# Half tiles of the gate phases: three excursions in the first and last block, and the shape of PV beside PV

## The chip, the cores and the metric

The kernel runs on one core of one Trainium2 chip, as one launch. The metric is device time in microseconds (us) of one execution, as the median of several runs. TensorE does the matmuls, VectorE (DVE) and ScalarE (ACT) read its results from PSUM, GpSimd (POOL) masks and scales in SBUF, and SyncE (SP) issues most of the DMAs.

## The reference

The input has 2048 tokens of 448 features. They are normalised once, and two branches read the result: causal attention in a sliding window of 256 with 16 heads of 28 features, and a gated feed-forward part with 1792 hidden features. Both are added to the input.

```python
xn = _layernorm(x, axis=-1)
return x + _A_ref(xn, A_wqkv, A_wo) + _B_ref(xn, B_w_gate, B_w_up, B_w_down)

# A: q, k, v = xn @ wqkv, by heads; scores = q k^T * Dh ** -0.5, masked to 0 <= i - j < 256
#    softmax(scores) @ v, by heads, then @ wo
# B: (gelu(xn @ w_gate) * (xn @ w_up)) @ w_down
```

## The kernel before

The tokens are cut into four blocks of 512 (`qb` 0 to 3). Each block has an attention phase and then a gate phase, in the order of the program; every engine runs its own instructions strictly in that order. In an attention phase, scores, exponentials and PV (the product of the probabilities with v, L560) are mixed by hand-written feeds with other dense work: the projections of the next block (`gen_proj`), the output products of the block before (`gen_down`), and in blocks 0 and 3 some of the up products ahead of time (`gen_up`). Which pairs are done ahead stands in `early`: f = 2, 4, 8 in block 0, and 2, 4, 6, 8, 10 in block 3; none in blocks 1 and 2.

The gate phase (`gated`, L412) goes over the 14 slices of 128 hidden features in pairs f = 0, 2, ..., 12. The 448 input features are 3 x 128 + 64. So a product of a slice is three dense matmuls (`three`, L228, array shape 128x128) and one half tile over the last 64 features (`half`, `mm_half`, L233, array shape 64x128). Half tiles come in pairs, one on the upper and one on the lower 64 rows of the array, which run at the same time. A pair f that is not early has two gate products and two up products, and so four half tiles; an early pair has only its gate products, two half tiles. To go from dense matmuls to half tiles and back is called an excursion here. To have few of them, the half tiles of two pairs are put together: `a`, whose dense part has just been issued, ends with its half tiles (`stop`), and `b` begins with them (`start`) and does its dense part afterwards.

```python
for fs in ((0,), (2, 4), (6, 8), (10, 12)):
    a = begin(fs[0])
    dense(a, True)
    ...
    halves(a, False)
    if b: halves(b, True)
    else: last_v()
    end(a)
```

So there are four excursions in a block: f = 0 alone, followed by the block's last PV (`last_v`, which is `rest` of `attention` and calls `pv(3)`), then 2 and 4, 6 and 8, 10 and 12. PV runs in array shape 64x32 in blocks 1 to 3 (48 matmuls, eight places of the array), and in 128x32 in block 0. Its result goes to SBUF through `add_halves` in blocks 1 to 3 (a copy on ScalarE, L548, and an addition on VectorE, L549), and through one copy on VectorE in block 0 (L570).

`end` applies Gelu on ScalarE to the two gate products at once (L452, tile `gt`, two banks) and multiplies with the up products on VectorE (L456, or L454 where they are already in `hT`). It then calls `hook`, which places other work behind each pair: the sums and scalings of the last heads (`after`), and in blocks 0 and 1 the normalisation of later tokens with their DMA transposes, and DMAs of packed k rows.

PSUM has eight banks. In the gate phase two tiles of two banks each (pool tag "s") take turns for `gt`, and four single banks (tags "m" twice, "o", "d") hold the up products and PV's result. A tile is taken again only when its reader is done: with the two `gt` tiles, a pair waits for the Gelu of the pair before the last. `turn` gives the order in which "o" and "d" are used, and `last_tag` hands it on to the output products that follow.

Of the kernel before, what the change touches and what calls it, by code (L numbers as in the profile page):

```python
# [8 lines left out]
ACT = mybir.ActivationFunctionType  # L9
ALU = mybir.AluOpType  # L10
AX = mybir.AxisListType
bf16 = mybir.dt.bfloat16
f32 = mybir.dt.float32
# [3 lines left out]
P = 128  # L17
NT = S // P
NF = F // P
QB, NB = 512, 4  # L20
# [55 lines left out]
def kernel(  # L76
# [11 lines left out]
    nc = tc.nc  # L88
# [6 lines left out]
    psum = fast.enter_context(tc.tile_pool(name="psum", bufs=2, space=bass.MemoryType.PSUM))  # L95

    phase = [None]
# [82 lines left out]
    xnT = const.tile([P, 4, S], bf16, name="xnT")  # L180
# [47 lines left out]
            nc.tensor.matmul(ps, lhsT=lhs(c), rhs=rhs(c), start=start and c == 0, stop=stop and c == 2,  # L228
                             skip_group_check=True)

    def mm_half(ps, lhs, rhs, hi, start, stop):
        p0 = 64 * hi
        nc.tensor.matmul(ps, lhsT=lhs[p0:p0 + 64], rhs=rhs[p0:p0 + 64], start=start, stop=stop,  # L233
                         tile_position=(p0, 0), skip_group_check=True)

    done = set()
    ring = [("m", "m", "d"), 0]
# [11 lines left out]
    def v_half(t, pv):  # L249
        mm_half(pv, xnT[:, 3, t * P:(t + 1) * P], wv[:, 3, :], t % 2, False, True)  # L250
# [22 lines left out]
    def qk_halves(qb, g, pq, pk):  # L273
        w3 = w3p[:, 4 * g:4 * g + 4, :].rearrange("p h d -> p (h d)")
        for hi, ps in enumerate((pq, pk)):
            mm_half(ps, w3, xnT[:, 3, qb * QB:(qb + 1) * QB], hi, False, True)
# [108 lines left out]
        hT = blk.tile([P, NF, QB], bf16, name="hT", tag="hT")  # L385
        hTs[qb] = hT

    def half(ps, f, gate, hi, ts, start, stop):

        w3 = wgu3 if gate != bool(hi) else wug3  # L390
        mm_half(ps, w3[:, f * P:(f + 1) * P], xnT[:, 3, ts], hi, start, stop)

    def three(ps, f, gate, ts, start, stop):
        w = wg if gate else wu
        mm3(ps, lambda c: w[:, c, f * P:(f + 1) * P], lambda c: xnT[:, c, ts], start, stop)

    def gen_up(qb, fs):

        ts = slice(qb * QB, (qb + 1) * QB)
        for f in fs:  # L400
            us = []
            for i in range(2):
                us.append(bank("ue"))
                three(us[i][:, :], f + i, False, ts, True, False)
                yield (650, HOLD) if i else 650
            for i in range(2):
                half(us[i][:, :], f + i, False, i, ts, False, True)
            for i in range(2):
                nc.vector.tensor_copy(out=hTs[qb][:, f + i, :], in_=us[i][:, :])  # L409
            yield -360  # L410

    def gated(qb, early, last_v, hook):  # L412

        ts = slice(qb * QB, (qb + 1) * QB)
        hT = hTs[qb]
        turn = ["o" if down_tag[0] == "d" else "d", down_tag[0]] * 4

        def begin(f):
            last_tag[0] = turn[0] if f not in early else last_tag[0]
            pr = dict(f=f, gt=phase[0].pool.tile([P, 2, QB], f32, name="gt", tag="s"), us=[])  # L420
            if f not in early:
                alone = (turn.pop(0), 1)
                tags = (("m", 2), alone)
                if qb == 0 and f == 0:
                    nxt = [ring[0][(ring[1] + i) % 3] for i in range(2)]
                    tags = [(x, 2 if x == "m" else 1) for x in nxt]
                    if "d" in nxt:
                        turn.insert(0, "o")
                for tag, n in tags:
                    pr["us"].append(psum.tile([P, QB], f32, name="u0", tag=tag, bufs=n))  # L430
            return pr

        def dense(pr, start):
            f = pr["f"]
            gs = [(pr["gt"][:, i, :], f + i, True) for i in range(2)]
            us = [(u[:, :], f + i, False) for i, u in enumerate(pr["us"])]
            for ps, fi, gate in (gs + us if f else us + gs):
                three(ps, fi, gate, ts, start, not start)

        def halves(pr, start):  # L440
            f = pr["f"]
            for i in range(2):
                if pr["us"]:
                    half(pr["gt"][:, i, :], f + i, True, 0, ts, start, not start)
                    half(pr["us"][i][:, :], f + i, False, 1, ts, start, not start)
                else:
                    half(pr["gt"][:, i, :], f + i, True, i, ts, start, not start)

        def end(pr):
            f = pr["f"]  # L450
            ge = work.tile([P, 2, QB], bf16, name="ge", bufs=2)
            nc.scalar.activation(out=ge[:, :, :], in_=pr["gt"][:, :, :], func=ACT.Gelu_apprx_tanh)  # L452
            if not pr["us"]:
                nc.vector.tensor_tensor(out=hT[:, f:f + 2, :], in0=ge[:, :, :], in1=hT[:, f:f + 2, :], op=ALU.mult)  # L454
            for i, u in enumerate(pr["us"]):
                nc.vector.tensor_tensor(out=hT[:, f + i, :], in0=ge[:, i, :], in1=u[:, :], op=ALU.mult)  # L456
            hook(f)

        for fs in ((0,), (2, 4), (6, 8), (10, 12)):
            a = begin(fs[0])  # L460
            dense(a, True)
            b = begin(fs[1]) if len(fs) > 1 else None
            halves(a, False)
            if b:
                halves(b, True)
            else:
                last_v()
            end(a)
            if b:
                dense(b, False)  # L470
                end(b)

    def steps_of(qb):

# [266 lines left out]
    for qb in range(NB):  # L741
# [13 lines left out]
        else:  # L755
            ring[0] = ("m",)
            tags = "dodo" if last_tag[0] == "o" else "odod"
# [16 lines left out]
        def hook(f):  # L774
            after(f)
            if qb < 3 and f == 4:
                collect(qb + 1)
            if qb < 3 and f == 10:
                deliver(qb + 1)
            if f >= 4 and qb < 2:  # L780
                t = 4 * qb + 4 + f // 2
                if f < 12:
                    norm(t + 2)
                    dma_transp(t + 2)
                    if qb == 0:
                        stat(t + 6)

        gated(qb, early, rest, hook)
        if qb < NB - 1:
            nc.scalar.preload_act_table_set("natural_log_exp_and_others")  # L790
# [138 lines left out]
```

## Time and profile before

| | |
|---|---|
| median of 3 runs | 223.92 us (223.68 to 224.28) |
| profiled execution | span 222.5 us from first to last instruction; no other time is recorded for it |
| mean granted clock of TensorE | 0.994 |
| TensorE matmuls | 2215, busy 211.6 us |
| TensorE weight loads | 2240, busy 94.5 us, beside matmuls |
| VectorE | 370 instructions, busy 156.3 us |
| ScalarE | 129 instructions, busy 132.9 us |
| GpSimd | 65 instructions, busy 44.7 us |
| gate phases | about 38.2 to 56.3 (block 0), 84.9 to 108 (1), 136 to 160 (2), 188 to 203.3 (3) |

Matmuls overlap one another: a dense one over 512 columns is listed with 0.38 us, and the next one starts before it has ended. So what counts is the distance from start to start, and not the length. Some records of matmuls are missing in a trace; a row then has a smaller count than the program and a gap of one matmul. Times inside the profile are counted from the first instruction.

### The profile page before, as it was taken

How to read it: one execution, taken by the hardware profiler on the slowest of the kernel's cores; microseconds unless marked ns; L12 is line 12 of the kernel's file. 1: busy time of each engine (PE TensorE's matmuls, PEld its weight loads, DVE VectorE, ACT ScalarE, POOL GpSimd, SP SyncE). 2: the span in 40 equal slices, each digit the busy share in tenths (PEclk: the TensorE clock that was granted, in tenths of full speed). 3: DMA queues.
4: the chain of work that ended last, by engine and by line, in shares of the span. 5: the costliest groups of instructions: out<-in, count | busy, mean ns of one | idle time of the engine just before them, and what ended most of it. 6: DMA issues, size and time to landing. Idle time of an engine off the chain costs nothing.

```text
span 222.5 us, 5330 instructions
## 1 busy us (share of the span) xinstructions
PE 211.6 (95%) x2215; PEld 94.5 (42%) x2240; DVE 156.3 (70%) x370; ACT 132.9 (60%) x129; POOL 44.7 (20%) x65
## 2 busy tenths in 40 slices
PE   6899999999999999999999999999999999999990
PEld 2333333344444454444444445444444435434470
DVE  5989996799666983778566895585454999479210
ACT  4597788644878874533868886323767778453000
POOL 5763687320000220022000030022000022022000
PEclk9999999999999999999999999999999999999997
DMA  6994899104100001001500001200000000000011
GB/s 190 312 327 47 195 327 289 20 2 72 45 3 21 24 24 31 16 19 28 70 0 24 24 0 45 43 0 0 0 4 24 24 0 24 21 0 4 22 45 27
DMA packets 18046, 13.31 MB, mean 60 GB/s; under 512 B 8704, under 2 KB 16992, under 8 KB 18016
## 3 DMA queue, kind: packets, MB, share of 16 engines
q1 hardware_dynamic: 17072, 12.62, 21.6%
q8 instruction: 19, 0.31, 0.6%
q10 hardware_dynamic: 944, 0.29, 0.5%
q14 instruction: 11, 0.09, 0.2%
HBM read 9.15 MB, written 2.18 MB: 51 GB/s over the span
## 4 chain that ended last, share of the span: by engine, by line
PE 91%; DVE 4%; issue 1%; DMA 1%; ACT 0%; DVEq 0%
PE po L375 20%; PE gt L228 17%; PE u L228 12%; PE sc L600 6%; PE po L370 6%; PE gt L233 5%; PE ue L228 5%; PE ov L560 5%; PE pq L228 4%; PE pv L228 4%; PE pk L228 3%; PE pq L233 2%; DVE st L195 1%; PE ue L233 1%; DMA x_sb<-in_A_x_dram 1%
## 5 line engine op out<-in xcount | busy, mean ns | idle before, releaser
L604 ACT ACTIVATE p_sb<-sc 128x2048 bf16<-128x2048 f32 (+2 forms) x42 | 73.8, 1758 | 12.6 <-PE sc L600 7.3
L375 PE MATMUL po<-wd,hT 128*128 128x448 bf16 (+1 forms) x238 | 50.0, 342 | 0.0
L452 ACT ACTIVATE ge<-gt 128x1024 bf16<-128x1024 f32 x28 | 28.7, 1024 | 33.6 <-PE u L233 20.9
L527 POOL TENSOR_TENSOR oN<-oc,l 128x512 bf16<-128x512 f32 x12 | 16.0, 1333 | 138.6 <-DVE l L544 88.2
L228 PE MATMUL gt<-xnT,wg 128*128 128x512 bf16 x161 | 38.9, 380 | 1.0 <-issue 0.9
L456 DVE TENSOR_TENSOR hT<-ge,u 128x512 bf16<-128x512 bf16 x40 | 25.6, 682 | 9.7 <-ACT ge L452 9.6
L375 PEld LDWEIGHTS <-hT 128*128 128x128 bf16 x238 | 21.4, 98 | 18.6 <-issue 2.6
L228 PE MATMUL u<-xnT,wu 128*128 128x512 bf16 x116 | 28.8, 379 | 0.2
L508 DVE TENSOR_TENSOR p_sb<-p_sb,masks 128x256 bf16<-128x256 bf16 (+1 forms) x90 | 27.2, 356 | 0.4 <-ACT p_sb L604 0.4
L228 PEld LDWEIGHTS <-wg 128*128 128x128 bf16 x168 | 15.1, 98 | 21.5 <-issue 5.2
L228 PEld LDWEIGHTS <-wu 128*128 128x128 bf16 x168 | 16.0, 98 | 19.2 <-issue 1.0
L549 DVE TENSOR_TENSOR oc<-oc,ov 128x512 f32<-128x512 f32 x12 | 8.3, 688 | 18.3 <-ACT oc L548 18.3
L600 PE MATMUL sc<-qT,kT 28*64 28x320 bf16 (+7 forms) x640 | 16.9, 263 | 0.1
L380 DVE TENSOR_TENSOR res<-po,x_sb 128x448 bf16<-128x448 f32 (+1 forms) x17 | 9.9, 585 | 8.7 <-PE po L375 8.6
L370 PE MATMUL po<-wo,oN 128*128 128x448 bf16 (+1 forms) x68 | 15.9, 343 | 0.0
L518 POOL TENSOR_SCALAR_AFFINE_SELECT p_sb<-p_sb 128x512 bf16<-128x512 bf16 (+1 forms) x20 | 14.2, 731 | 8.3 <-ACT p_sb L604 8.1
L409 DVE CAST hT<-ue 128x512 bf16<-128x512 f32 x16 | 10.2, 680 | 6.3 <-PE ue L233 6.2
L548 ACT COPY oc<-ov 128x512 f32<-128x512 f32 x12 | 7.0, 584 | 11.9 <-PE ov L560 11.9
L233 PE MATMUL gt<-xnT,wgu 64*128 64x512 bf16 x48 | 13.2, 379 | 0.0
L228 PE MATMUL pq<-xnT,wqp 128*128 128x512 bf16 x36 | 11.7, 380 | 0.7 <-DVE v_sb L253 0.3
L534 DVE STREAM_TRANSPOSE l<-oc 128x512 f32<-128x512 f32 x16 | 11.3, 704 | 1.4 <-POOL oN L527 1.2
L228 PE MATMUL ue<-xnT,wu 128*128 128x512 bf16 x43 | 11.6, 380 | 0.4 <-issue 0.2
(87 smaller groups left out, 235.4 us busy)
## 6 DMA issues: line engine op xcount, KB each, us to landing
out_dram<-res SPq DMA_DIRECT2D x15, 112.0 KB
x_sb<-in_A_x_dram SPq DMA_DIRECT2D x3, 448.0 KB
wu<-in_B_w_up_dram SPq DMA_DIRECT2D x1, 1344.0 KB
wg<-in_B_w_gate_dram SPq DMA_DIRECT2D x1, 1344.0 KB
wd<-in_B_w_down_dram SPq DMA_DIRECT2D x3, 448.0 KB
wraw<-in_A_wqkv_dram SPq DMA_DIRECT2D x2, 252.0 KB
wo<-in_A_wo_dram SPq DMA_DIRECT2D x4, 98.0 KB
wv<-in_A_wqkv_dram SPq DMA_DIRECT2D x1, 336.0 KB
```

What stands on the lines that cost most here:

```text
L228: nc.tensor.matmul(ps, lhsT=lhs(c), rhs=rhs(c), start=start and c == 0, stop=stop and c == 2, skip_group_check=True)
L233: nc.tensor.matmul(ps, lhsT=lhs[p0:p0 + 64], rhs=rhs[p0:p0 + 64], start=start, stop=stop, tile_position=(p0, 0), skip_group_check=True)
L370: nc.tensor.matmul(po[:, 0:w], lhsT=oN[:, g, cs], rhs=wo[:, g, lo:up], start=(g == 0), stop=False, skip_group_check=True)
L375: nc.tensor.matmul(po[:, 0:w], lhsT=hT[:, f, cs], rhs=wd[:, f, lo:up], start=False, stop=(f == NF - 1), skip_group_check=True)
L452: nc.scalar.activation(out=ge[:, :, :], in_=pr["gt"][:, :, :], func=ACT.Gelu_apprx_tanh)
L456: nc.vector.tensor_tensor(out=hT[:, f + i, :], in0=ge[:, i, :], in1=u[:, :], op=ALU.mult)
L508: nc.vector.tensor_tensor(out=reg, in0=reg, in1=m, op=ALU.mult)
L518: nc.gpsimd.affine_select(out=reg, in_=reg, pattern=mid + [[1 if diag else -1, min(w, P)]], compare_op=ALU.is_ge, fill=0.0, base=0 if diag ...
L527: nc.gpsimd.tensor_tensor(out=oN[:, g, :], in0=oc[:, :], in1=inv, op=ALU.mult)
L534: nc.vector.transpose(out=l1[:, :, :].rearrange("p a b -> p (a b)"), in_=oc[:, :])
L600: nc.tensor.matmul(ss[k0:k0 + nk, j, col:col + nq], lhsT=kT[r, g, kt * P + k0:kt * P + k0 + nk], rhs=qT[r, g, qb * QB + q0:qb * QB + q0 + ...
L604: nc.scalar.activation(out=p_sb[:, :, 0:ncol], in_=ss[:, :, 0:ncol], func=ACT.Exp, scale=SCALE)
```

## The change

In blocks 0 and 3 the pairs are grouped as (0, 2), (4, 8, 6), (10, 12), which makes three excursions; blocks 1 and 2 keep their four. In a group of three the middle one (f = 8, early in both blocks) takes two single banks for its gate products in place of a `gt` tile (`apart`), and its Gelu is two instructions of one bank each. The half tiles of the group that stands beside PV (f = 0, and f = 2 with it in block 3) are issued in blocks 1 to 3 as four matmuls of 32 columns each, which is PV's array shape 64x32; in block 0 they keep 64x128. The order of the pairs, and with it of `hook`, becomes 0, 2, 4, 8, 6, 10, 12 in blocks 0 and 3.

```diff
-    def mm_half(ps, lhs, rhs, hi, start, stop):
+    def mm_half(ps, lhs, rhs, hi, start, stop, m=P):
         p0 = 64 * hi
-        nc.tensor.matmul(ps, lhsT=lhs[p0:p0 + 64], rhs=rhs[p0:p0 + 64], start=start, stop=stop,
-                         tile_position=(p0, 0), skip_group_check=True)
+        for c in range(0, P, m):
+            nc.tensor.matmul(ps[c:c + m], lhsT=lhs[p0:p0 + 64, c:c + m], rhs=rhs[p0:p0 + 64], start=start, stop=stop,
+                             tile_position=(p0, c), skip_group_check=True)
...
+        def single(name, tag):
+            return psum.tile([P, QB], f32, name=name, tag=tag, bufs=2 if tag == "m" else 1)[:, :]
+
-        def begin(f):
+        def begin(f, apart=False):
             last_tag[0] = turn[0] if f not in early else last_tag[0]
-            pr = dict(f=f, gt=phase[0].pool.tile([P, 2, QB], f32, name="gt", tag="s"), us=[])
+            pr = dict(f=f, us=[])
+            if apart:
+                pr["gs"] = [single("g0", tag) for tag in ("m", turn.pop(0))]
+                return pr
+            pr["gt"] = phase[0].pool.tile([P, 2, QB], f32, name="gt", tag="s")
+            pr["gs"] = [pr["gt"][:, i, :] for i in range(2)]
...
         def end(pr):
             f = pr["f"]
             ge = work.tile([P, 2, QB], bf16, name="ge", bufs=2)
-            nc.scalar.activation(out=ge[:, :, :], in_=pr["gt"][:, :, :], func=ACT.Gelu_apprx_tanh)
+            if "gt" in pr:
+                nc.scalar.activation(out=ge[:, :, :], in_=pr["gt"][:, :, :], func=ACT.Gelu_apprx_tanh)
+            else:
+                for i, g in enumerate(pr["gs"]):
+                    nc.scalar.activation(out=ge[:, i, :], in_=g, func=ACT.Gelu_apprx_tanh)
...
-        for fs in ((0,), (2, 4), (6, 8), (10, 12)):
-            a = begin(fs[0])
-            dense(a, True)
-            b = begin(fs[1]) if len(fs) > 1 else None
-            halves(a, False)
-            if b:
-                halves(b, True)
-            else:
+        for fs in ((0, 2), (4, 8, 6), (10, 12)) if qb in (0, 3) else ((0,), (2, 4), (6, 8), (10, 12)):
+            prs = [begin(fs[0])]
+            dense(prs[0], True)
+            prs += [begin(f, len(fs) == 3 and f == fs[1]) for f in fs[1:]]
+            for pr in prs:
+                halves(pr, pr is not prs[0], 32 if qb and not fs[0] else P)
+            if not fs[0]:
                 last_v()
-            end(a)
-            if b:
-                dense(b, False)
-                end(b)
+            end(prs[0])
+            for pr in prs[1:]:
+                dense(pr, False)
+                end(pr)
```

More of the change, by code (lines that the diff above doesn't have):

```diff
@@ L386, in new_hT, with half @@
         hTs[qb] = hT
-    def half(ps, f, gate, hi, ts, start, stop):
+    def half(ps, f, gate, hi, ts, start, stop, m=P):
         w3 = wgu3 if gate != bool(hi) else wug3
-        mm_half(ps, w3[:, f * P:(f + 1) * P], xnT[:, 3, ts], hi, start, stop)
+        mm_half(ps, w3[:, f * P:(f + 1) * P], xnT[:, 3, ts], hi, start, stop, m)
     def three(ps, f, gate, ts, start, stop):
@@ L416, in gated @@
         turn = ["o" if down_tag[0] == "d" else "d", down_tag[0]] * 4
-        def begin(f):
+        def single(name, tag):
+            return psum.tile([P, QB], f32, name=name, tag=tag, bufs=2 if tag == "m" else 1)[:, :]
+        def begin(f, apart=False):
             last_tag[0] = turn[0] if f not in early else last_tag[0]
-            pr = dict(f=f, gt=phase[0].pool.tile([P, 2, QB], f32, name="gt", tag="s"), us=[])
+            pr = dict(f=f, us=[])
[4 more added lines that the diff above has]
+            pr["gs"] = [pr["gt"][:, i, :] for i in range(2)]
             if f not in early:
-                alone = (turn.pop(0), 1)
-                tags = (("m", 2), alone)
+                tags = ("m", turn.pop(0))
                 if qb == 0 and f == 0:
-                    nxt = [ring[0][(ring[1] + i) % 3] for i in range(2)]
-                    tags = [(x, 2 if x == "m" else 1) for x in nxt]
-                    if "d" in nxt:
+                    tags = [ring[0][(ring[1] + i) % 3] for i in range(2)]
+                    if "d" in tags:
                         turn.insert(0, "o")
-                for tag, n in tags:
-                    pr["us"].append(psum.tile([P, QB], f32, name="u0", tag=tag, bufs=n))
+                pr["us"] = [single("u0", tag) for tag in tags]
             return pr
@@ L434, in dense, with halves @@
             f = pr["f"]
-            gs = [(pr["gt"][:, i, :], f + i, True) for i in range(2)]
-            us = [(u[:, :], f + i, False) for i, u in enumerate(pr["us"])]
+            gs = [(g, f + i, True) for i, g in enumerate(pr["gs"])]
+            us = [(u, f + i, False) for i, u in enumerate(pr["us"])]
             for ps, fi, gate in (gs + us if f else us + gs):
                 three(ps, fi, gate, ts, start, not start)
-        def halves(pr, start):
+        def halves(pr, start, m):
             f = pr["f"]
@@ L443, in halves @@
                 if pr["us"]:
-                    half(pr["gt"][:, i, :], f + i, True, 0, ts, start, not start)
-                    half(pr["us"][i][:, :], f + i, False, 1, ts, start, not start)
+                    half(pr["gs"][i], f + i, True, 0, ts, start, not start, m)
+                    half(pr["us"][i], f + i, False, 1, ts, start, not start, m)
                 else:
-                    half(pr["gt"][:, i, :], f + i, True, i, ts, start, not start)
+                    half(pr["gs"][i], f + i, True, i, ts, start, not start, m)
         def end(pr):
@@ L455, in end @@
             for i, u in enumerate(pr["us"]):
-                nc.vector.tensor_tensor(out=hT[:, f + i, :], in0=ge[:, i, :], in1=u[:, :], op=ALU.mult)
+                nc.vector.tensor_tensor(out=hT[:, f + i, :], in0=ge[:, i, :], in1=u, op=ALU.mult)
             hook(f)
-        for fs in ((0,), (2, 4), (6, 8), (10, 12)):
-            a = begin(fs[0])
-            dense(a, True)
-            b = begin(fs[1]) if len(fs) > 1 else None
-            halves(a, False)
-            if b:
-                halves(b, True)
-            else:
+        for fs in ((0, 2), (4, 8, 6), (10, 12)) if qb in (0, 3) else ((0,), (2, 4), (6, 8), (10, 12)):
[5 more added lines that the diff above has]
+            if not fs[0]:
                 last_v()
-            end(a)
-            if b:
-                dense(b, False)
-                end(b)
+            end(prs[0])
+            for pr in prs[1:]:
+                dense(pr, False)
+                end(pr)
     def steps_of(qb):
```

## Prediction

> **What bounds the kernel now.** I read the page first: the engine totals, then the chain that ended last.
>
> ```profile
> PE 211.6 (95%) x2215; PEld 94.5 (42%) x2240; DVE 156.3 (70%) x370; ACT 132.9 (60%) x129; POOL 44.7 (20%) x65
> ...
> PE 91%; DVE 4%; issue 1%; DMA 1%; ACT 0%; DVEq 0%
> ```
>
> TensorE is busy for 95% of the span and is 91% of the chain, so a tenth of a microsecond taken from its queue moves the end by as much, unless a wait takes its place. The change edits only that queue's order and shapes in the gate phases, so next I read the timeline of TensorE through block 3's gate phase (start us, length us, line, output and inputs, array shape, moving shape, count), and after it ScalarE's rows of the same stretch.
>
> ```profile
> 189.25 1.46 PE L228 MATMUL gt<-xnT,wg 128*128 128x512 bf16 x6
> 190.64 0.39 PE L233 MATMUL gt<-xnT,wgu 64*128 64x512 bf16 x1
> ...
> 190.87 0.38 PE L233 MATMUL gt<-xnT,wgu 64*128 64x512 bf16 x1
> ...
> 191.18 0.74 PE L560 MATMUL ov<-p_sb,v_sb 64*32 64x256 bf16 x48
> 192.08 1.24 PE L228 MATMUL gt<-xnT,wg 128*128 128x512 bf16 x5 [0.16 <-issue]
> 193.25 0.39 PE L233 MATMUL gt<-xnT,wgu 64*128 64x512 bf16 x1
> ...
> 193.66 0.37 PE L233 MATMUL gt<-xnT,wgu 64*128 64x512 bf16 x1
> ...
> 193.98 2.76 PE L228 MATMUL gt<-xnT,wg 128*128 128x512 bf16 x12
> 196.68 0.39 PE L233 MATMUL gt<-xnT,wgu 64*128 64x512 bf16 x1
> ...
> 196.91 0.38 PE L233 MATMUL gt<-xnT,wgu 64*128 64x512 bf16 x1
> ...
> 197.22 2.76 PE L228 MATMUL gt<-xnT,wg 128*128 128x512 bf16 x12
> ```
>
> ```profile
> 192.10 0.58 ACT L548 COPY oc<-ov 128x512 f32<-128x512 f32 x1 [2.91 <-PE ov L560]
> 192.58 2.13 ACT L452 ACTIVATE ge<-gt 128x1024 bf16<-128x1024 f32 x2
> ```
>
> The pitch of dense matmuls is (2.76 - 0.38)/11 = 0.216 us. Anything beyond one pitch between starts is a switch of array shape or a wait. Twelve dense matmuls from 193.98 would be followed at 193.98 + 12 x 0.216 = 196.57; the half tiles start at 196.68, 0.10 late. Two half tiles run abreast in a pitch: two pairs are 0.43, and the next dense one starts at 197.22 where 196.57 + 0.43 = 197.00 was due. So **one excursion of half tiles costs about 0.21 us** besides its work, some 0.10 at each end.
>
> From the last pair (190.87) to PV (191.18) is 0.31: **the switch from 64x128 to PV's 64x32 costs 0.09**. The 192.08 row holds five of the six matmuls of f=2 (one record is missing), so the first stood a pitch earlier, at 191.86.
>
> One real wait stands in this phase: the second pair at 193.66 comes 0.41 after the first, 0.41 - 0.22 = 0.19 late. It is f=4's first use of the two-bank tile that f=0's Gelu must leave, and that Gelu stands on ScalarE behind the copy of PV's result: PV starts at 191.18, the copy at 192.10, and f=0's Gelu runs to about 193.6 (two Gelus of 1.02 with a pause between). **The tile is free 193.66 - 191.18 = 2.48 after PV's start.**
>
> **The change part by part.**
>
> *Block 0, three excursions.* The half tiles of f=0 and f=2 now share one excursion, followed by PV as before; f=4, 8, 6 share the next; f=10, 12 stay. One excursion goes: -0.21. I looked for a wait in its place. Here the result of PV is copied by VectorE, so ScalarE runs f=0's Gelu ahead of it, as this view of the same stretch of block 0 shows:
>
> ```profile
> 41.58 1.02 ACT L452 ACTIVATE ge<-gt 128x1024 bf16<-128x1024 f32 x1 [0.89 <-PE gt L233]
> 42.60 0.69 DVE L570 COPY oc<-ov 128x512 f32<-128x512 f32 x1 [1.39 <-POOL oN L527]
> 43.21 1.27 DVE L456 TENSOR_TENSOR hT<-ge,u 128x512 bf16<-128x512 bf16 x2
> ```
>
> f=4's dense part would start about 43.5 (f=2's start at 42.02 in the trace, plus one pair 0.22, plus six pitches 1.30), and its tile is free at 42.6: no wait. From there in pitches: f=4 dense to 44.8, the switch 0.1, half tiles of f=4 (0.22), f=8 at 45.1, f=6 at 45.4 (two pairs, 0.43); dense f=8 from 45.9 to 47.2, f=6 (twelve, 2.59) to 49.8, f=10 to 52.4; half tiles of f=10 from 52.5, of f=12 at 52.9, its second pair at 53.1. f=8's two single banks, PV's old one among them (copied by 43.3), and f=6's banks, f=0's old ones (free with the products at 44.5), are there in time. The tightest is f=12, which takes f=6's banks: VectorE does f=8's product (0.65), norm (0.60) and statistics (0.62 + 0.18) from about 49.0 to 51.0, then f=6's two products (1.28) to 52.3, and the second bank is wanted at 53.1. Margin 0.8; if that cover went, by VectorE being as much as one such round of 1.4 late, the loss would be 0.6. Splitting f=8's Gelu in two adds one ScalarE start, at most 2 x 0.58 - 1.02 = 0.14 by the copy of one bank, beside dense work. The DMAs issued in hook keep their order but for tokens 9 and 10 exchanged; token 9's transpose goes out near 53 rather than 51, and TensorE wants it at 58.6: nothing. Value -0.21; bounds -0.21 and +0.4.
>
> *Blocks 1 and 2, half tiles in 64x32.* Four matmuls become sixteen, 24 added in the two blocks. No row shows 64x512 in this shape. The nearest is PV: 48 matmuls, in sum 10,240 columns, which eight abreast at the pitch's rate (0.216/512) are 0.54; from its start 191.18 to the next dense matmul at 191.86 are 0.68, and 0.14 of that is the drain out. So PV runs eight abreast, and 16 x 512/8 columns are 0.43, as now. The switch of 0.09 goes: -0.09 a block, -0.18 for both. Bounds: -0.20 (a little skew saved too) and, four abreast, +0.43 - 0.09 = +0.34 a block.
>
> *Block 3, both.* One excursion fewer, -0.21, and 64x32 for the 24 matmuls of f=0 and f=2, -0.09: -0.30. But **the wait grows**. PV starts 0.22 - 0.09 = 0.13 later, behind f=2's half tiles, so at 191.31, and the tile of f=0 is free 2.48 later, at 193.79. TensorE leaves PV at 191.99, does f=2's six dense matmuls (1.30, to 193.28), and now comes straight to f=4's dense part, which needs that tile: a wait of 0.50 where 0.19 was. Before, f=2's own excursion lay in that gap. Net -0.30 + 0.31 = +0.01: nothing. Behind this wait is all of TensorE's queue; later tiles are free in time (f=2's Gelu follows f=0's by 1.02 and ends near 194.8, f=6 wants that tile at 193.79 + 1.30 + 0.10 + 0.43 = 195.6; f=6's dense part ends near 198.5 and its Gelu by 199.7, f=12 wants that tile 1.30 + 0.10 + 0.22 after 198.5, at 200.1). Bounds: -0.49 (no wait at all) and +0.1.
>
> The sum is -0.21 - 0.18 + 0.01 = **-0.38 us**: the span goes from 222.5 to 222.1. The profiled execution gives no time but its span; the median of the runs, 223.92, lies 1.4 above it, which I leave as it is: 223.5, or 0.17% less. Some 0.3% (0.67 us) is what a measurement can tell from no change.
>
> A rule that speaks against the 64x32 shape: in PV's stretch matmuls start 0.68/48 = 14 ns apart on the average. By the Trainium skill (TensorE: Matmul & The Clock Gate, "Wait — 56ns, not 53.3ns?") matmul starts never come closer than about 25 ns; by that floor the 42 added matmuls would be some 1.05 us of issue, an estimate, and the sum 224.6. The trace does not agree, PV's 14 ns being below it.
>
> **The rivals.**
>
> *The wait does not grow* (0.16). If block 3's Gelu came before the copy, or f=4's dense part could start while f=0's tile is read, the wait would stay 0.19 or vanish: -0.69 to -0.88, so 223.0 to 223.2. For it: a single wait of 0.3 us decides. Against: the copy at 192.10 stands ahead of the Gelu, and the 193.66 row waits for exactly that tile.
>
> *The half tiles in 64x32 run four abreast* (0.14), the slower one. PV's four column tiles stream four different parts of p_sb; here four column tiles stream the same rows of xnT, 512 long. If these don't overlap, the 56 matmuls (16 + 16 + 24) take fourteen pitches rather than seven: +7 x 0.216 = 1.5 us, giving 225.0. It turns the sign from 0.38 on, and passes the bound from 1.05, five of the seven rounds doubled. Against: PV's 48 eight abreast.
>
> *Issue is the bound* (0.04): 42 added matmuls at PV's 14 ns are +0.6, giving 224.1.
>
> *The switch stays between half tiles and PV* (0.05), so that the shape does nothing: +0.27 against the forecast, 223.8.
>
> *Block 0's cover goes* (0.04): VectorE 1.4 late, giving 223.5 + 0.6 = 224.1.
>
> **How the numbers follow.** The forecast has 0.57. Its own spread is 0.25 us (the waits are read to 0.05, the medians run over 0.6), so I put 0.15 of it beyond 223.25. Faster: 0.15 + 0.16 = 0.31. Within: 0.42 + 0.04 + 0.05 + 0.04 = 0.55. Slower: 0.14. Range: down to the first rival less a bit of spread, 222.9, up to the 224.1 cases with theirs, 224.4; the 225.0 case is left out.
>
> **What would show it.** Right: in blocks 1 to 3 no step above one pitch between the last half tile and PV, and eight of them starting within some 25 ns; one excursion fewer in blocks 0 and 3; in block 3 a wait of about 0.5 ahead of f=4's dense part, named Gelu, and the dense part of f=12 starting as long after f=0's as before. Wrong: 0.43 between rounds of half tiles; a wait for VectorE ahead of f=12's half tiles in block 0; no wait at f=4.

## The result and the profile after

| | before | after |
|---|---|---|
| median of 21 runs each | 224.22 us | 223.62 us |
| ratio to before | | 0.9975, 95% interval 0.9967 to 0.9983 |
| span of the profiled execution | 222.5 us | 221.9 us |

The change gains 0.25%, 0.56 us (0.38 to 0.74 by the interval). The forecast was 223.5 us and a gain of 0.38 us. The kernel before has a median of 224.22 us here, in 21 runs, where its three earlier runs gave 223.92. The page of the changed kernel reads much as before, with the same share of TensorE in the chain that ended last. It has 67 more matmul records: 42 are the matmuls that the change adds (2282 weight loads in place of 2240), and the other 25 are records that the trace of before lacks.

```profile
PE 212.9 (96%) x2282; PEld 95.3 (43%) x2282; DVE 156.0 (70%) x370; ACT 133.1 (60%) x131; POOL 44.8 (20%) x65
...
PE 91%; DVE 3%; ACT 2%; DMA 1%; issue 0%; ACTq 0%
```

The span holds more than the gate phases, so I compare each gate phase by itself, from its first half tile to the first output product behind it. This is TensorE's timeline through block 3 of the changed kernel, and behind it, from the kernel before, the row at which its phase ended.

```profile
190.17 0.40 PE L234 MATMUL gt<-xnT,wgu 64*32 64x512 bf16 x4
190.19 0.40 PE L234 MATMUL u<-xnT,wgu 64*32 64x512 bf16 x4
190.40 0.39 PE L234 MATMUL gt<-xnT,wgu 64*32 64x512 bf16 x4
...
190.62 0.39 PE L234 MATMUL gt<-xnT,wgu 64*32 64x512 bf16 x4
...
190.83 0.73 PE L569 MATMUL ov<-p_sb,v_sb 64*32 64x256 bf16 x48
191.50 1.47 PE L228 MATMUL gt<-xnT,wg 128*128 128x512 bf16 x6
193.30 1.46 PE L228 MATMUL gt<-xnT,wg 128*128 128x512 bf16 x6 [0.34 <-ACT ge L459]
...
202.79 0.92 PE L371 MATMUL po<-wo,oN 128*128 128x448 bf16 x4
```

```profile
203.27 0.92 PE L370 MATMUL po<-wo,oN 128*128 128x448 bf16 x4
```

The three rounds of quartered half tiles start at 190.17, 190.40 and 190.62, and PV starts at 190.83: each step is about one pitch of 0.22 and the step of 0.31 ahead of PV is gone. A round is two rows of four matmuls each, 0.01 to 0.02 apart, and its eight starts lie within some 0.03 us, so eight do run abreast. Then comes the wait. Six dense matmuls from 191.50 would be followed at 191.50 + 6 x 0.216 = 192.80; f=4's dense part starts at 193.30, **0.50 late**, and the row names the Gelu. (Its 0.34 is only the time in which no matmul was under way.) ScalarE in the same stretch:

```profile
191.74 0.58 ACT L557 COPY oc<-ov 128x512 f32<-128x512 f32 x1 [3.02 <-PE ov L569]
192.22 1.95 ACT L459 ACTIVATE ge<-gt 128x1024 bf16<-128x1024 f32 x2
```

The copy of PV's result still stands ahead of f=0's Gelu, which ends at 192.22 + 1.02 = 193.24. The whole phase is 202.79 - 190.17 = 12.62, and was 203.27 - 190.64 = 12.63 (12.62 before rounding, 0.01 above the changed kernel's).

Block 0 has no wait. In the changed kernel's timeline the dense matmuls of f=2 and f=4 follow each other without a step, the three pairs 4, 8 and 6 share one excursion, and the output products start at 56.00.

```profile
40.83 0.39 PE L234 MATMUL gt<-xnT,wgu 64*128 64x512 bf16 x1
...
42.18 2.76 PE L228 MATMUL gt<-xnT,wg 128*128 128x512 bf16 x12
44.88 0.39 PE L234 MATMUL gt<-xnT,wgu 64*128 64x512 bf16 x1
...
45.85 1.47 PE L228 MATMUL g<-xnT,wg 128*128 128x512 bf16 x6
...
56.00 0.54 PE L371 MATMUL po<-wo,oN 128*128 128x448 bf16 x2
```

The same phase in the kernel before:

```profile
40.88 0.39 PE L233 MATMUL gt<-xnT,wgu 64*128 64x512 bf16 x1
...
56.26 0.54 PE L370 MATMUL po<-wo,oN 128*128 128x448 bf16 x2
```

That is 56.00 - 40.83 = 15.17, against 56.26 - 40.88 = 15.38 before. Block 1 begins and ends as follows, before and then after:

```profile
87.86 0.39 PE L233 MATMUL gt<-xnT,wgu 64*128 64x512 bf16 x1
...
107.85 0.54 PE L370 MATMUL po<-wo,oN 128*128 128x448 bf16 x2
```

```profile
87.60 0.40 PE L234 MATMUL gt<-xnT,wgu 64*32 64x512 bf16 x4
...
107.49 0.54 PE L371 MATMUL po<-wo,oN 128*128 128x448 bf16 x2
```

Blocks 1 and 2 give 19.89 against 19.99 each. So the four gate phases have lost 0.21, 0.10, 0.10 and 0.01 us, **0.42 in all**.

The spans differ by 0.6. To see where the rest lies, take the start of the last addition to the result on VectorE, before and then after:

```profile
217.34 0.39 DVE L380 TENSOR_TENSOR res<-po,x_sb 128x224 bf16<-128x224 f32 x1 [1.33 <-PE po L375]
```

```profile
216.85 0.39 DVE L381 TENSOR_TENSOR res<-po,x_sb 128x224 bf16<-128x224 f32 x1 [1.33 <-PE po L376]
```

From block 0's first half tile it is 217.34 - 40.88 = 176.46 before and 216.85 - 40.83 = 176.02 after. So the 0.42 reaches the end of the work whole, and little is added to it. Ahead of this stretch and behind it the traces differ where the code does not: in the eleven traces of this study, block 0's first half tile stands at 40.72 to 41.06, and the span ends some 4.5 to 5.4 after the last addition starts.

### The profile page after: what moved, and what is told of

Read it like the earlier page. It is cut to its first block, busy times and chain, and to the rows that moved or that the text cites. A ratio compares the mean times of both kernels' runs of the same rounds, so it can differ in the third digit from the quotient of the medians.

```text
span 221.9 us, 5442 instructions
## 1 busy us (share of the span) xinstructions
PE 212.9 (96%) x2282; PEld 95.3 (43%) x2282; DVE 156.0 (70%) x370; ACT 133.1 (60%) x131; POOL 44.8 (20%) x65
## 3 DMA queue, kind: packets, MB, share of 16 engines
q1 hardware_dynamic: 17072, 12.62, 22.5%
## 4 chain that ended last, share of the span: by engine, by line
PE 91%; DVE 3%; ACT 2%; DMA 1%; issue 0%; ACTq 0%
PE po L376 20%; PE gt L228 15%; PE u L228 12%; PE sc L609 6%; PE po L371 6%; PE gt L234 5%; PE ue L228 5%; PE ov L569 5%; PE pq L228 4%; PE pv L228 4%; PE pk L228 3%; PE pq L234 2%; PE g L228 1%; DVE st L195 1%; PE ue L234 1%; DMA x_sb<-in_A_x_dram 1%
## 5 line engine op out<-in xcount | busy, mean ns | idle before, releaser
L459 ACT ACTIVATE ge<-gt 128x1024 bf16<-128x1024 f32 x26 | 26.5, 1024 | 32.5 <-PE u L234 20.1
L228 PE MATMUL gt<-xnT,wg 128*128 128x512 bf16 x156 | 37.7, 380 | 0.3 <-ACT ge L459 0.3
L234 PE MATMUL gt<-xnT,wgu 64*128 64x512 bf16 (+1 forms) x67 | 12.7, 380 | 0.0
L228 PE MATMUL pq<-xnT,wqp 128*128 128x512 bf16 x45 | 12.2, 380 | 0.3 <-DVE v_sb L254 0.3
```

What stands on the lines that cost most here:

```text
L234: nc.tensor.matmul(ps[c:c + m], lhsT=lhs[p0:p0 + 64, c:c + m], rhs=rhs[p0:p0 + 64], start=start, stop=stop, tile_position=(p0, c), skip_gr ...
```

## The experiments

The ratios below are to the kernel before, each with its 95% interval. The lengths of gate phases are read as above; where their code is the same they repeat from trace to trace to 0.01 us, so they tell apart what the timed runs, with intervals of 0.18 us and more to each side, can't.

### The shape alone

```diff
-        for fs in ((0, 2), (4, 8, 6), (10, 12)) if qb in (0, 3) else ((0,), (2, 4), (6, 8), (10, 12)):
+        for fs in ((0,), (2, 4), (6, 8), (10, 12)):
```

> The grouping of before in all blocks (four excursions each), with the half tiles of f=0 in 64x32 ahead of PV in blocks 1 to 3. Theory (TensorE's queue alone sets the end; each step costs what the two traces show): the switch of 0.09 to 0.10 us goes three times, -0.3 us against the kernel before (ratio 0.9987), and block 3 keeps its wait of 0.19 at f=4's half tiles. Rival 1 (what is saved before PV comes back as a longer wait for the PV copy or a Gelu): no change, ratio 1.000, with the wait in block 3 grown to about 0.28. Rival 2 (all of the change's gain is the shape): ratio 0.9975.

Measured: ratio 0.9982 (0.9973 to 0.9991). The gate phases of blocks 1 to 3 are 0.10 shorter each, block 0's is as before. In block 3 the second pair of half tiles stands 0.40 after the first, 0.41 in the kernel before: the wait did not grow, since it is counted from PV's start and all moved together. The shape is worth 0.31 us in the trace, on its own, and rival 1 is out. Rival 2, the shape as the whole gain, is not told apart by the ratio, whose interval holds 0.9975; the 0.21 of block 0 in the trace is what speaks against it.

### The grouping alone

```diff
-                halves(pr, pr is not prs[0], 32 if qb and not fs[0] else P)
+                halves(pr, pr is not prs[0], P)
```

> The change's grouping with all half tiles in 64x128 as before. Theory: block 0 gains one excursion, 0.21; block 3 gains one and its wait ahead of f=4 stays 0.50 against 0.19, so it loses 0.1; blocks 1 and 2 are as before. Sum -0.1 us against the kernel before (ratio 0.9995), 0.3 above the change. Rival (the grouping is what brings the change's gain): ratio 0.9980 or less.

Measured: ratio 0.9997 (0.9988 to 1.0005), which leaves the rival out. Block 0's phase is 0.21 shorter, block 3's 0.10 longer, with the wait of 0.50 ahead of f=4. So the grouping brings next to nothing as a whole: what it wins in block 0 it half loses in block 3.

### Block 3's grouping undone

```diff
-        for fs in ((0, 2), (4, 8, 6), (10, 12)) if qb in (0, 3) else ((0,), (2, 4), (6, 8), (10, 12)):
+        for fs in ((0, 2), (4, 8, 6), (10, 12)) if qb == 0 else ((0,), (2, 4), (6, 8), (10, 12)):
```

> The change with block 3's grouping undone: groups of three excursions in block 0 only, 64x32 ahead of PV in blocks 1 to 3. Theory: block 3's grouping buys one excursion (0.21) and pays it with a longer wait (0.50 against 0.19), so undoing it gains 0.1 us: -0.51 against the kernel before (ratio 0.9977), 0.1 us below the change. Rival (the grouping of block 3 is worth its excursion): 0.2 us above the change, ratio about 0.9985.

Measured: ratio 0.9968 (0.9956 to 0.9981). Block 3's phase is 12.52, 0.10 below the change's 12.62. By the trace, the change would be better without its grouping in block 3. The timed ratio points the same way, but its interval overlaps the change's.

### The Gelu ahead of the copy in block 3

The change, with the Gelu call taken out of `end` into a function `gelu`, and called ahead of `last_v` in block 3; `end` does the rest where it did.

```diff
             if not fs[0]:
+                if qb == 3:
+                    gelu(prs[0])
                 last_v()
```

> The change, and in block 3 the Gelu of f=0 stands ahead of the copy of PV's result on ScalarE (only these two change places). Theory: the wait of 0.50 ahead of f=4's dense part is made by that copy; it goes whole, since the Gelu then ends near 191.9 and the dense part is due near 192.8: -0.9 us against the kernel before (ratio 0.9959), 0.5 below the change. Rival 1 (the wait is for something else, PV's bank or VectorE): wait and time as in the change, ratio 0.9975. Rival 2 (the wait goes but the copy, now up to 0.2 later, holds up VectorE's sums and with them the scaled heads that the last output products read): the wait of 0.50 comes back near 203 ahead of the output products.

Measured: ratio 0.9953 (0.9939 to 0.9967), median 223.06 us, the lowest of this study. All engines' timeline in block 3:

```profile
190.89 0.73 PE L576 MATMUL ov<-p_sb,v_sb 64*32 64x256 bf16 x48
190.95 1.02 ACT L458 ACTIVATE ge<-gt 128x1024 bf16<-128x1024 f32 x1 [2.18 <-PE gt L234]
...
191.55 2.76 PE L228 MATMUL gt<-xnT,wg 128*128 128x512 bf16 x12
191.87 0.58 ACT L564 COPY oc<-ov 128x512 f32<-128x512 f32 x1
...
200.83 1.62 POOL L543 TENSOR_TENSOR oN<-oc,l 128x512 bf16<-128x512 f32 x1 [2.48 <-DVE l L560]
...
202.34 0.92 PE L371 MATMUL po<-wo,oN 128*128 128x448 bf16 x4
```

The Gelu runs beside PV and ends at 191.97, and the twelve dense matmuls of f=2 and f=4 now follow each other without a step. The phase is 12.12 (before rounding), 0.50 shorter than the change's: the whole wait. From block 0's first half tile to the last addition are 175.53 us, so this 0.50 reaches the end too. The copy starts 0.98 after PV's start, 0.07 later than in the change, and rival 2's late cost does not come: the last scaled heads are done at 202.45, and the fourth of the output products that read them is due after 202.34 + 3 x 0.19 = 202.9.

### The same order in the kernel before

The kernel before's grouping and shape, with the same `gelu(prs[0])` ahead of `last_v()` in block 3.

> The grouping and the shape of before, and in block 3 the Gelu of f=0 ahead of the copy of PV's result on ScalarE. Theory: the one wait of the kernel before, 0.19 at f=4's half tiles, goes: -0.19 us (ratio 0.9992). Rival (the wait was for something else): no change, wait still there.

Measured: ratio 0.9987 (0.9976 to 0.9999). TensorE's timeline shows the second pair of half tiles one pitch behind the first; it stood 0.41 behind.

```profile
193.11 0.39 PE L234 MATMUL gt<-xnT,wgu 64*128 64x512 bf16 x1
...
193.33 0.38 PE L234 MATMUL gt<-xnT,wgu 64*128 64x512 bf16 x1
```

Block 3's phase is 12.43 against 12.62: 0.19. The wait in the kernel before, and the larger one that the change made of it, are the same thing.

### Block 3's grouping without the wait

The Gelu ahead of the copy, and block 3 with its four excursions:

```diff
-        for fs in ((0, 2), (4, 8, 6), (10, 12)) if qb in (0, 3) else ((0,), (2, 4), (6, 8), (10, 12)):
+        for fs in ((0, 2), (4, 8, 6), (10, 12)) if qb == 0 else ((0,), (2, 4), (6, 8), (10, 12)):
```

> The version with block 3's Gelu of f=0 ahead of PV's copy, and block 3's grouping undone (four excursions there). Theory: with no wait left in either, the grouping of block 3 is worth its whole excursion, so this one is 0.21 us above the version with both, -0.7 against the kernel before (ratio 0.9968), block 3's phase from the first half tile to the output products 0.21 longer. Rival (the Gelu's place alone brought the gain, and the grouping brings nothing even without a wait): as fast as the version with both, ratio 0.9959.

Measured: ratio 0.9969 (0.9957 to 0.9981). Block 3's phase is 12.33 against 12.12 with the grouping. So with the wait gone the excursion is worth its 0.21 in block 3 too: the grouping was right, and lacked one line. The timed ratio lies above the 0.9953 of the version with both, as expected, but the intervals overlap; it is the trace that shows the 0.21.

### The Gelu first in blocks 1 and 2 as well

```diff
-                if qb == 3:
+                if qb:
                     gelu(prs[0])
```

> The change with the Gelu of f=0 ahead of PV's copy in blocks 1, 2 and 3, not in 3 alone. Theory: an order of ScalarE is worth only the wait of TensorE that it takes away; the traces show none in blocks 1 and 2, so their gate phases keep their length to 0.02 us and the time is that of the version with block 3 alone (ratio 0.9955). Rival (the copy, up to 0.2 later, delays the sums of the last heads, which the next attention phase's output products read): blocks 1 and 2 lengthen by up to 0.2 each.

Measured: ratio 0.9953 (0.9939 to 0.9967), gate phases 19.89 in blocks 1 and 2, as without it. There f=2 has up products too, twelve dense matmuls in place of six, and these cover the copy and the Gelu. The order is worth only the wait that it takes away.

### Seven excursions in blocks 1 and 2

```diff
-        for fs in ((0, 2), (4, 8, 6), (10, 12)) if qb in (0, 3) else ((0,), (2, 4), (6, 8), (10, 12)):
+        for fs in ((0, 2), (4, 8, 6), (10, 12)) if qb in (0, 3) else ((0,), (2,), (4,), (6,), (8,), (10,), (12,)):
```

> The change, with blocks 1 and 2 undone the other way: every pair has its own excursion there, seven instead of four. Theory: three excursions more in each of two blocks at 0.21 are +1.24 us against the change; against the kernel before -0.42 + 1.24 = +0.8 (ratio 1.0037). Rival 1 (excursions are hidden in part by waits that these blocks have anyway): less than +0.6 against the change. Rival 2 (pairs alone come so soon after one another that TensorE waits for banks): more than +1.8, with gaps named Gelu or the products in the gate phases of blocks 1 and 2.

Measured: ratio 1.0095 (1.0080 to 1.0111), that is 1.2% or 2.7 us above the change, where 1.24 was expected. The gate phases of blocks 1 and 2 are 20.51 against 19.89: 0.62 longer each for three excursions, 0.207 apiece, as expected. The rest lies behind the gate phase, a place that neither rival named. TensorE, and then ScalarE, at the start of block 2's attention phase:

```profile
108.31 0.55 PE L371 MATMUL po<-wo,oN 128*128 128x448 bf16 x2
109.53 0.42 PE L609 MATMUL sc<-qT,kT 28*64 28x320 bf16 x16 [0.67 <-ACT ge L459]
```

```profile
108.46 1.02 ACT L459 ACTIVATE ge<-gt 128x1024 bf16<-128x1024 f32 x1 [2.21 <-PE u L234]
```

A pair alone ends with its half tiles, so the last Gelu can start only at 108.46, behind the end of all of TensorE's gate work. In the usual group the last pair has its half tiles first and its up products last, and its Gelu runs beside those. The first scores of the next phase need the PSUM of that Gelu. They were due two output products and a switch after 108.31, at 108.31 + 2 x 0.19 + 0.09 = 108.78, and come at 109.53: a wait of 0.75 a block. From block 1's first half tile to block 2's are 53.00 us, and 51.49 in the change; of these 1.51 the excursions are 0.62, this wait 0.75, and 0.14 comes at the second group of scores: it starts at 112.72, just after the phase's first exponential, which runs from 110.80 for 1.88 and so ends at 112.68. In the change this exponential ends at 110.66, ahead of the second scores' turn at 110.98. From block 2's first half tile to block 3's the trace has 1.38 more than the change, so the two blocks make 2.89, and the timed runs gave 2.7. Rival 2's price was right, its place and its releaser's cause were not.

### All half tiles in 64x32

```diff
-                halves(pr, pr is not prs[0], 32 if qb and not fs[0] else P)
+                halves(pr, pr is not prs[0], 32)
```

> The change with every half tile of the gate phases in 64x32, in all blocks, not only those beside PV: 92 half tiles become 368 matmuls, where the change has 14 that become 56. Theory: eight run abreast whatever stands beside them, a round takes one pitch, so the excursions cost what they did: time as the change, within 0.1 us; in block 0 too, since 64x32 and PV's 128x32 there are still two shapes. Rival 1 (matmuls that stream the same rows are slowed): 39 more rounds; if each were a pitch longer, +8 us, a tenth of a pitch +0.8. Rival 2 (issue is the bound at 14 ns each): no change in the rounds, since eight times 14 ns is below a pitch.

The count there is off: the gate phases have 96 half tiles, so 384 matmuls and 41 more rounds. Measured: ratio 0.9998 (0.9982 to 1.0014), where the change has 0.9975 (0.9967 to 0.9983): about 0.5 us slower rather than equal, though the intervals just touch. TensorE's timeline in block 1's second excursion:

```profile
91.41 0.40 PE L234 MATMUL gt<-xnT,wgu 64*32 64x512 bf16 x4
91.43 0.40 PE L234 MATMUL u<-xnT,wgu 64*32 64x512 bf16 x4
91.64 0.39 PE L234 MATMUL gt<-xnT,wgu 64*32 64x512 bf16 x4
...
92.07 0.39 PE L234 MATMUL gt<-xnT,wgu 64*32 64x512 bf16 x4
...
92.40 1.47 PE L228 MATMUL gt<-xnT,wg 128*128 128x512 bf16 x6
```

The rounds keep their pitch (91.41, 91.64, and the fourth at 92.07), so rival 1 is out: matmuls that stream the same rows don't slow each other. But the whole excursion, first half tile to next dense matmul, is 92.40 - 91.41 = 0.99 where the change has 0.97 for the same work in 64x128. The eight places of a round start one after the other, the second row 0.02 after the first. Each phase is 0.04 to 0.06 longer, 0.19 in all. Between the gate phases the trace shows no other step. At the very end it shows one: the last addition on VectorE starts at 217.69, after 2.00 us of idle time that a DMA of an earlier result ended, where the change has 1.33, ended by TensorE. The traces of the shape alone and of block 3's grouping without the wait show a smaller wait of this kind (1.60 and 1.59), so it does not need the quartered half tiles, and one trace can't tell whether they make it longer. So of the timed difference to the change 0.19 us is explained here, and the rest stays open.

## Why the prediction was right, point by point

**The price of an excursion, 0.21.** Shown: block 0 lost one and is 0.21 shorter, six more in blocks 1 and 2 lengthen their phases by 0.207 each, and block 3 loses 0.21 where nothing waits.

**The switch ahead of PV, 0.09 a block.** The mechanism was right and the size a little small: the traces have 0.10, since PV's own stretch, 191.50 - 190.83 = 0.67, is also 0.01 shorter without the switch ahead of it (191.86 - 191.18 = 0.68 before). The lower bound of -0.20 for blocks 1 and 2 was the value. Rounds of eight took one pitch, so the slower rival (four abreast), the rival on issue and the one of a switch that stays are out. The 25 ns between matmul starts that was cited from the Trainium skill (TensorE: Matmul & The Clock Gate, "Wait — 56ns, not 53.3ns?") does not hold for the places of a 64x32 array: the eight matmuls of a round start within some 0.03 us, 3 to 4 ns apart.

**Block 3's wait, 0.50 where 0.19 was.** Met to 0.01, and its cause shown by the Gelu's place: the wait leaves with the copy. The net of block 3 was +0.01 and is -0.01, the difference being mostly the switch. What was to follow from it holds too: f=12's dense part starts 11.41 us after f=0's gate products, 11.42 before.

**Block 0's cover.** It held; no step stands ahead of f=12's half tiles. One small bound was too low: the two Gelus of one bank take 0.597 us each and one Gelu of two banks 1.024, which makes 2 x 0.597 - 1.024 = 0.17 more, where at most 0.14 was allowed. It lies beside dense work and costs nothing, as was said.

**The sum.** -0.38 was forecast, the traces' gate phases give -0.42, and the timed runs -0.56 (-0.38 to -0.74). The forecast lies at that interval's edge and the trace's sum within it. That 223.5 us was met within 0.12 is in part luck: the median of before came out 0.30 higher than in the three runs from which the forecast counted, and 0.38 below 224.22 would have been 223.84. What the timed runs have beyond 0.42, if anything, no row shows; the parts of the trace ahead of the first gate phase and behind the last addition differ by more than that excess of 0.14 among kernels that have the same code there. The faster rival, in which the wait does not grow, is met by a changed kernel only: with the Gelu first it went to 0.9953.

## What to carry to other kernels

On a chain that is one engine's queue from end to end, starts counted in pitches give steps of a tenth of a microsecond their price and place, where timed runs can't. When work is regrouped to save a switch, look at what the moved work was covering: six dense matmuls were too short for a copy and a Gelu, and the saved 0.21 came back as 0.31. A releaser that stands behind unrelated work in its own engine's order can be the cheapest thing to move: one instruction put first took 0.50 us off the changed kernel, more than the change's own 0.42. In the kernel before the same move took 0.19, since less was waiting there.

## What the runs showed of the hardware

Splitting a 64x128 half tile into four matmuls of 64x32 costs nothing in the rounds, also where all four stream the same rows (eight of them start 0.21 to 0.23 us after the eight before), and some 0.02 us an excursion in stagger. Counted from the start of the last matmul of the old shape, and beyond its pitch, a change of array shape cost 0.09 to 0.10 us at each of the boundaries between dense matmuls and half tiles (128x128 to 64x128 or 64x32, and back) and from 64x128 to PV's 64x32, with TensorE's granted clock at 0.99 to 1.0 of full speed.
